# Shifting the activations by 32 bytes in SBUF: x and gg from 64 to 32 modulo 256

## The chip, the cores and the metric

The kernel runs on one core of a Trainium2 chip. The metric is the device time of one execution in microseconds. Three executions of the kernel before took 1003.8 to 1005.95 us, with a median of 1004.16 us.

## What is computed

Attention with a memory term, and then two feed-forward networks one behind the other, all in float32. This is the reference without its setup:

```python
scores = scale * q @ k.T;  causal mask;  a = softmax(scores);  local = a @ v
mem_out = (phi(q) @ M_prev) / (phi(q) . z_prev + 1e-06)
x = g * mem_out + (1 - g) * local          # 2304 tokens x 512
h = x @ w_in;   x = (s * max(h, 0)**2 + b) @ w_out          # layer 1, d_ff 2048
h = x @ w2_in
g = where(h >= 1, h, where(h <= -1, 0, (h + 1)**2 / 4))     # layer 2, d_ff 2048
out = g @ w2_out
```

## The kernel before

**Two halves of each number.** The large products run on TensorE as float32r. Each operand is split into a high and a low part, and each product is taken as three matmuls: high times high, high times low, low times high. So a matmul here reads a moving operand (the activations, 256 or 512 columns of 4 bytes in each of 128 partitions) and a stationary one (128 columns of weights, loaded by an LDWEIGHTS ahead of it).

**Stages.** From about 0 to 520 us attention (`att`) and layer 1 (`layer1`) are interleaved block by block after the table `ORDER`; a block is 256 tokens. The last block of layer 1 has 512 tokens ("wide", about 524 to 617 us). Layer 2 (`layer2`) follows to the end: its first products run by Strassen's scheme (`product`, lines 1181 to 1183, 256 columns; `plain`, lines 1235 to 1237, for the 256-token block), its second products (`second`, lines 1213, 1214, 1220; in `plain` lines 1252, 1254, 1255) have 512 columns.

**Which operand lies where.** Layer 1's first product (`h_mms`, lines 951 to 953) moves `xx`, which holds x in its high and low parts; the second (`layer1_step`, lines 1014, 1015 and 1019) moves `gg`, in the wide block alternately `gg` and `g2`. `product` moves the sums that layer 2 puts into `xx` and `gg` (`xo`), `plain` moves `xp`. The second products of layer 2 move weights (`wo`), with the activations as the stationary operand. The weights of all three are in tiles `wi` and `wo`.

Tiles are placed in SBUF one behind the other in the order in which the program makes them, each rounded up to 32 bytes. Tiles named `before_x`, `after_x` and `before_g2` hold nothing: they are there to set addresses. All offsets within these tiles at which a matmul of 256 or 512 columns begins are multiples of 1024 bytes (2048 for weights that move), so an operand's start modulo 256 is that of its tile. The start addresses per partition, modulo 256, as the built programs have them:

| tiles | what | before | after |
|---|---|---|---|
| `wi`, `wo`, `stg` | weights, staging | 128 | 128 |
| `xx` | x; layer 2's sums | 64 | 32 |
| `ident`, `zr`, `con` | constants | 128 | 96 |
| `mask`, `rr`, `gg` | mask; layer 1's activations | 64 | 32 |
| `qk`, `nv`, `zb`, `ee`, `uz` | attention's inputs, first steps | 64 | 32 |
| `pt`, `aa`, `at`, `au`, `av` | attention's scores and their transposes | 192 | 160 |
| `xp`, `xr`, `raw`, `st` | layer 2's inputs, staging of its weights | 64 | 32 |
| `g2` | layer 1's wide block; layer 2 | 128 | 128 |

The order of all instructions is worked out ahead by a planner (`Plan`) from a table of costs; every engine then runs its list in that order. Addresses are no part of that table.

Of the kernel before, what the change touches and what calls it, by code (L numbers as in the profile page):

```python
# [9 lines left out]
F32 = mybir.dt.float32  # L10
# [7 lines left out]
P = 128  # L18
# [357 lines left out]
def tile_kernel(ctx: ExitStack, tc: tile.TileContext, qk_in, nv_in, z_prev, beta,  # L376
# [16 lines left out]
    def t32(shape, name):  # L393
        return pool[0].tile(list(shape), F32, name=name)

    def t32r(shape, name):
        return pool[0].tile(list(shape), F32R, name=name)
# [17 lines left out]
    def w_out_part(i, j):  # L415
        return part("wo", i, j)
    stg_t = [t32([P, DM], f"stg{i}") for i in range(4)]
    t32([P, 48], "before_x")
    xx = t32r([P, 2 * NK * XC], "xx")
    xh = [xx[:, i * XC:(i + 1) * XC] for i in range(NK)]  # L420
    xl = [xx[:, (NK + i) * XC:(NK + i + 1) * XC] for i in range(NK)]
# [24 lines left out]
    TILES = [{}, {}]  # L446

    def pool_of(i, n, *parts):

        units = []  # L450
        for j in range(n):
            names = [f"{name}{i}{j}" for name, _, _ in parts]
            TILES[i].update({x: (shape, dt) for x, (_, shape, dt) in zip(names, parts)})
            units.append((lambda x=names[0]: made[x]) if len(names) == 1 else (lambda x=names: tuple(made[y] for y in x)))
        return Pool(units)
# [20 lines left out]
    TILES[1]["xr"] = ([P, NK * 2 * T], F32)  # L476
    R_RAW2 = pool_of(1, 3, ("raw", [P, 2 * DM], U32))
    R_STG2 = pool_of(1, 6, ("st", [P, DM], F32))
    TILES[1]["before_g2"] = ([P, 16], F32)
    TILES[1]["g2"] = ([P, 8 * T], F32R)  # L480


# [894 lines left out]
```

## Time and profile before

| what | value |
|---|---|
| median of three executions | 1004.16 us |
| the profiled execution, its own time | 1006.14 us |
| its span, first to last instruction | 1004.4 us |
| TensorE matmul busy | 992.5 us, 99% of the span |
| weight loads, beside the matmuls | 878.5 us |
| VectorE, ScalarE, GpSimd busy | 660.0, 589.0, 206.3 us |
| granted TensorE clock, mean | 0.995 |
| HBM traffic | 114 GB/s over the span |

The profiled execution's own time is 1.7 us above its span. Matmuls overlap in the records (the recorded length of one reaches past the start of the next), so what a matmul costs is read from the distance between the starts of two that follow each other, called its pitch below.

### The profile page before, as it was taken

The page shows a single profiled execution, that of the slowest core. Times are in us where ns is not written, and L with a number is a line of the kernel's source. Part 1 is how long each engine was busy: PE and PEld are TensorE (multiplying, and loading weights), DVE is VectorE, ACT ScalarE, POOL GpSimd, SP SyncE. Part 2 cuts the span into 40 slices and gives each one's busy share as a digit, 9 for nine tenths or more (in the row PEclk, how much of TensorE's full clock was granted, in tenths as well). Part 3 has the DMA queues.
Part 4 walks back from the last instruction along what each step waited for, and adds up shares of the span by engine and source line. Part 5 has one row for each costly group of instructions (what it writes and reads, how often), then busy time and mean ns, then how long its engine had stood idle before and what let it go on. Part 6 is the DMA issues. An engine that isn't in the chain of part 4 may idle for free.

```text
span 1004.4 us, 19651 instructions
## 1 busy us (share of the span) xinstructions
PE 992.5 (99%) x7480; PEld 878.5 (87%) x7480; DVE 660.0 (66%) x1545; ACT 589.0 (59%) x1331; POOL 206.3 (21%) x320
## 2 busy tenths in 40 slices
PE   8999999999999999999999999999999999999998
PEld 7799998898898889789898888999899998999987
DVE  5899855635644545554687885788769555576742
ACT  5999876646656655565556555666546434254323
POOL 5411133211110211111132321232234101011100
PEclk8999999999999999999999999999999999999999
DMA  9491034211221211211043334634354971231301
GB/s 321 170 410 60 15 92 140 70 52 49 76 70 48 85 62 56 68 60 46 1 152 132 127 116 143 225 126 147 110 185 162 355 248 46 82 95 32 106 27 37
DMA packets 50718, 115.57 MB, mean 115 GB/s; under 512 B 5440, under 2 KB 16192, under 8 KB 50624
## 3 DMA queue, kind: packets, MB, share of 16 engines
q1 hardware_dynamic: 50400, 113.73, 33.2%
q8 instruction: 59, 0.97, 0.4%
q0 software_dynamic: 224, 0.59, 0.3%
q14 instruction: 35, 0.29, 0.1%
HBM read 87.56 MB, written 26.74 MB: 114 GB/s over the span
## 4 chain that ended last, share of the span: by engine, by line
PE 91%; ACT 3%; DVE 2%; DMA 2%; issue 1%; SPq 0%; POOL 0%; DVEq 0%; POOLq 0%; ACTq 0%
PE hb L951 6%; PE hb L953 6%; PE hb L952 6%; PE ab L826 6%; PE yb L1014 5%; PE yb L1019 5%; PE yb L1015 5%; PE ab L905 4%; PE ab L881 4%; PE yb L1213 3%; PE yb L1214 3%; PE yb L1220 3%; PE ab L1220 3%; PE ab L1213 3%; PE ab L1214 3%; PE ab L1182 3%
## 5 line engine op out<-in xcount | busy, mean ns | idle before, releaser
L951 PE MATMUL hb<-xx,wi 128*128 128x256 f32 (+1 forms) x512 | 152.7, 298 | 0.0
L952 PE MATMUL hb<-xx,wi 128*128 128x256 f32 (+1 forms) x512 | 149.5, 292 | 0.0
L953 PE MATMUL hb<-xx,wi 128*128 128x256 f32 (+1 forms) x512 | 149.5, 292 | 0.0
L1014 PE MATMUL yb<-gg,wo 128*128 128x256 f32 (+1 forms) x394 | 102.6, 292 | 1.5 <-ACT gg L537 1.2
L951 PEld LDWEIGHTS hb<-xx,wi 128*128 128x128 f32 x512 | 96.4, 188 | 7.0 <-issue 3.5
L952 PEld LDWEIGHTS hb<-xx,wi 128*128 128x128 f32 x512 | 96.3, 188 | 2.8
L953 PEld LDWEIGHTS hb<-xx,wi 128*128 128x128 f32 x512 | 96.2, 188 | 2.9
L1015 PE MATMUL yb<-gg,wo 128*128 128x256 f32 (+1 forms) x394 | 98.0, 281 | 0.0
L522 ACT ACTIVATE aa<-aa,sm 128x384 f32<-128x384 f32 (+4 forms) x112 | 69.4, 621 | 48.2 <-DVE sm L837 48.0
L529 DVE TENSOR_TENSOR gg<-rr,gg 128x256 fp32r<-128x256 f32 (+1 forms) x102 | 44.6, 439 | 74.6 <-ACT gg L537 56.1
L1014 PEld LDWEIGHTS yb<-gg,wo 128*128 128x128 f32 x394 | 74.1, 188 | 9.0 <-issue 3.6
L837 DVE CUSTOM_DVE_ANT_0 aa<-ab,mask 128x512 f32<-128x512 f32 (+3 forms) x112 | 59.1, 553 | 32.9 <-PE ab L826 32.7
L995 ACT ACTIVATE rr<-hb 128x256 f32<-128x256 f32 (+1 forms) x105 | 42.8, 408 | 55.8 <-PE hb L953 52.8
L1015 PEld LDWEIGHTS yb<-gg,wo 128*128 128x128 f32 x394 | 74.2, 188 | 0.5
L1019 PE MATMUL yb<-gg,wo 128*128 128x256 f32 (+1 forms) x394 | 69.3, 288 | 0.0
L826 PE MATMUL ab<-qk 64*64 64x512 f32 (+5 forms) x320 | 58.4, 472 | 0.0
L1019 PEld LDWEIGHTS yb<-gg,wo 128*128 128x128 f32 x394 | 54.5, 188 | 2.4 <-issue 1.8
L861 POOL TENSOR_SCALAR aa<-aa,sm 128x384 f32<-128x384 f32 (+4 forms) x41 | 25.3, 619 | 149.1 <-DVE sm L854 114.8
L1182 PE MATMUL ab<-xx,wi 128*128 128x256 f32 x196 | 55.2, 282 | 0.0
L1181 PE MATMUL ab<-xx,wi 128*128 128x256 f32 x196 | 55.1, 281 | 0.0
L1183 PE MATMUL ab<-xx,wi 128*128 128x256 f32 x196 | 55.1, 281 | 0.0
L1181 PE MATMUL hb<-xx,wi 128*128 128x256 f32 x188 | 52.8, 281 | 0.0
(337 smaller groups left out, 2843.1 us busy)
## 6 DMA issues: line engine op xcount, KB each, us to landing
w2d<-st SPq DMA_DIRECT2D x48, 256.0 KB, 4.1
nv<-in_nv_dram SPq DMA_DIRECT2D x16, 576.0 KB, 3.7
wir<-in_moe_w_in_dram SPq DMA_DIRECT2D x16, 512.0 KB, 10.2
wor<-in_moe_w_out_dram SPq DMA_DIRECT2D x16, 512.0 KB, 10.2
raw<-in_moe_w_in_dram SPq DMA_DIRECT2D x16, 512.0 KB, 3.9
raw<-in_moe_w_out_dram SPq DMA_DIRECT2D x16, 512.0 KB, 4.4
qk<-in_qk_dram SPq DMA_DIRECT2D x16, 448.0 KB, 3.3
wo<-w2d SPq DMA_DIRECT2D x12, 512.0 KB, 5.1
```

The lines of the kernel that those rows point to most:

```text
L522: nc.scalar.activation(o(), i(), func, **{a: b() if callable(b) else b for a, b in kw.items()})
L826: nc.tensor.matmul(zs[x].t[own if t == 4 else slice(0, n), at:at + c1 - c0], qk.t[own, q0:q0 + n], qk.t[own, k0 + c0:k0 + c1], start=True, ...
L951: nc.tensor.matmul(o, w_in_part(fi, 0)[:, kt, :], x_h(kt), start=kt == 0, stop=False)
L952: nc.tensor.matmul(o, w_in_part(fi, 0)[:, kt, :], x_l(kt), start=False, stop=False)
L953: nc.tensor.matmul(o, w_in_part(fi, 1)[:, kt, :], x_h(kt), start=False, stop=kt == NK - 1)
L1014: nc.tensor.matmul(yv(c), w_out_part(fi, 0)[:, cs], gg.t[0], start=fi == 0 and c % k == 0, stop=False)
L1015: nc.tensor.matmul(yv(c), w_out_part(fi, 1)[:, cs], gg.t[0], start=False, stop=False)
L1019: pe(c_mm(n), lambda c=c, cs=cs, gg=gg, fi=fi: nc.tensor.matmul(yv(c), w_out_part(fi, 0)[:, cs], gg.t[1], start=False, stop=fi == NF - 1 a ...
L1181: nc.tensor.matmul(o, sw(q, k, 0, kt), xo(k, 0, kt), start=j == 0 and kt == 0, stop=False)
L1182: nc.tensor.matmul(o, sw(q, k, 0, kt), xo(k, 1, kt), start=False, stop=False)
L1213: nc.tensor.matmul(y.t, gh.t[:, cs], wo2(q, i, 0), start=first and jj == 0, stop=False)
L1214: nc.tensor.matmul(y.t, gh.t[:, cs], wo2(q, i, 1), start=False, stop=False)
```

## The change

The pad ahead of `xx` loses 8 float32 (32 bytes per partition), and the pad ahead of `g2` gains as many. So every tile from `xx` to the last one ahead of `before_g2` begins 32 bytes lower, and `g2` and the weights stay where they are. In the addresses after, `xx`, `rr`, `gg`, `xp` and the others of the table are at an odd multiple of 32 bytes.

```diff
     stg_t = [t32([P, DM], f"stg{i}") for i in range(4)]
-    t32([P, 48], "before_x")
+    t32([P, 40], "before_x")
     xx = t32r([P, 2 * NK * XC], "xx")
...
-    TILES[1]["before_g2"] = ([P, 16], F32)
+    TILES[1]["before_g2"] = ([P, 24], F32)
     TILES[1]["g2"] = ([P, 8 * T], F32R)
```

No instruction is added, removed or moved on any engine: the five engines' lists are the same row by row, and only operand addresses differ.

## Rows read from the trace of the kernel before

**Rows 1.** The page's first two parts: busy time by engine; 40 slices
```profile
PE 992.5 (99%) x7480; PEld 878.5 (87%) x7480; DVE 660.0 (66%) x1545; ACT 589.0 (59%) x1331; POOL 206.3 (21%) x320
...
PEclk8999999999999999999999999999999999999999
```

**Rows 2.** What TensorE waited for: us in total, times, longest
```profile
PE ab L826 <- DMA wir<-in_qk_dram: 3.2, 2, 1.7
PE yb L1014 <- ACT gg L537: 1.2, 1, 1.2
PE hb L1309 <- DVE zr L562: 1.1, 1, 1.1
...
PE yb L1014 <- POOL gg L542: 0.3, 1, 0.3
```

**Rows 3.** TensorE in time, layer 1: start, recorded length (us), line
```profile
295.76 0.28 PE L953 MATMUL hb<-xx,wi 128*128 128x256 f32 x1
...
297.12 0.28 PE L1014 MATMUL yb<-gg,wo 128*128 128x256 f32 x1
```

**Rows 4.** The same view, another stretch of layer 1
```profile
82.11 0.28 PE L1015 MATMUL ab<-gg,wo 128*128 128x256 f32 x1
...
83.99 0.28 PE L953 MATMUL hb<-xx,wi 128*128 128x256 f32 x1
```

**Rows 5.** The same view, layer 2: Strassen products, then second products
```profile
819.79 0.28 PE L1182 MATMUL hb<-xx,wi 128*128 128x256 f32 x1
...
823.21 0.39 PE L1213 MATMUL yb<-wo,wo 128*128 128x512 f32 x1
...
825.93 1.07 PE L1220 MATMUL ab<-wo,wo 128*128 128x512 f32 x4
```

**Rows 6.** The same view, layer 1's wide block: g2 is printed g
```profile
574.54 0.39 PE L1014 MATMUL yb<-g,wo 128*128 128x512 f32 x1
...
577.26 0.39 PE L951 MATMUL hb<-xx,wi 128*128 128x512 f32 x1
...
582.86 0.39 PE L1014 MATMUL yb<-gg,wo 128*128 128x512 f32 x1
...
585.66 0.39 PE L1014 MATMUL yb<-g,wo 128*128 128x512 f32 x1
```

**Rows 7.** Busy us (x instructions) by stretch: PE, PEld, DVE, ACT, POOL; clock; DMA
```profile
83.00:89.00 6.00, 6.00 (x53) 6.00 (x53) 5.70 (x11) 6.00 (x16) 1.08 (x1) 1.00 0.00 0
376.00:382.00 6.00, 6.00 (x53) 6.00 (x52) 1.71 (x4) 2.89 (x8) 0.51 (x1) 1.00 0.17 67
812.00:818.00 6.00, 6.00 (x53) 6.00 (x52) 2.33 (x4) 1.08 (x3) 0.00 (x0) 1.00 0.95 310
```

**Rows 8.** Groups by line and shape: count, busy us, mean recorded ns
```profile
L952 PE MATMUL hb<-xx,wi 128*128 128x256 f32 x448 | 124.3, 277 | 0.0
...
L1015 PE MATMUL yb<-gg,wo 128*128 128x256 f32 x384 | 94.1, 278 | 0.0
...
L1182 PE MATMUL ab<-xx,wi 128*128 128x256 f32 x196 | 55.2, 282 | 0.0
...
L952 PE MATMUL hb<-xx,wi 128*128 128x512 f32 x64 | 25.2, 394 | 0.0
...
L1235 PE MATMUL ab<-xp,wi 128*128 128x256 f32 x24 | 6.7, 281 | 0.0
...
L1015 PE MATMUL yb<-gg,wo 128*128 128x512 f32 x10 | 3.9, 394 | 0.0
```

## The prediction

> **What bounds the kernel.** I read the share of busy time first, then what TensorE waited for, then the starts of single matmuls. TensorE is busy for 992.5 of 1004.4 us, and its granted clock is full in all slices but the first [rows 1]. All its waits for other engines and for transfers come to 7.4 us; the largest are 3.2 us for the first inputs, 1.2 us for one gg, 1.1 us for a constant at the very start [rows 2]. So TensorE's own list is the path from end to end: a nanosecond on the pitch of a matmul is a nanosecond on the span, times the count, and a nanosecond on another engine is mostly nothing.
>
> The change leaves each instruction in its place, so what it can alter is how long an instruction takes at another address. The question is whether the trace shows a pitch that goes by address. It does, in two ways.
>
> First, by address. In the wide block the same line, L1014, runs with gg (64 modulo 256) and with g2 (128). With g2, 12 matmuls of 512 columns take 577.26 - 574.54 = 2.72 us, a pitch of 0.2267 us; with xx, 24 take 582.86 - 577.26 = 5.60 us, 0.2333 us; with gg, 12 take 585.66 - 582.86 = 2.80 us, 0.2333 us again [rows 6]. So 64 costs 6.7 ns a matmul more than 128, at 512 columns. Layer 2's second products, whose moving weights are at 128, also have 0.2267 us (12 in 825.93 - 823.21 us) [rows 5].
>
> Second, by state. At 256 columns and one address, 64, there are two pitches. In one stretch of layer 1, 12 matmuls with xx and gg take 297.12 - 295.76 = 1.36 us: 0.1133 us, half of 0.2267 [rows 3]. In another, with the same two tiles, 16 take 83.99 - 82.11 = 1.88 us: 0.1175 us [rows 4]. In layer 2, 29 take 823.21 - 819.79 = 3.42 us: 0.1179 us [rows 5]. I take 0.1177 us for the slow pitch, 4.4 ns over the fast one. A run of matmuls settles in one pitch and keeps it until something else interrupts it. Load elsewhere does not decide it: the slow pitch stands with VectorE and ScalarE full and DMA idle, with them idle and DMA at 0.95, and with all of them light [rows 7].
>
> How many stand in each, counted from the starts in that same view (between the first and last rows shown in [rows 3, 4] for layer 1, and like [rows 5] for layer 2): of layer 1's 2688 matmuls of 256 columns, 1678 at 114.5 ns or less, 784 slow, the rest in between or at the end of a run. Of layer 2's 1536, 1515 are slow. The recorded lengths agree: 281 to 282 ns in layer 2, and 277 to 278 ns as layer 1's mixed mean, with 394 ns for xx and gg in the wide block [rows 8]. So the slow pitch costs now 784 x 4.4 ns = 3.4 us in layer 1, 1515 x 4.4 ns = 6.7 us in layer 2, and 252 x 6.7 ns = 1.7 us in the wide block (192 with xx, 60 with gg).
>
> **The change part by part.** The pad ahead of xx moves xx, gg and xp from 64 to 32, so all of the 4224 matmuls of 256 columns and these 252 of 512 start at an address that no matmul of the trace before has: none of its starts is an odd multiple of 32. It is an operation whose cost must be bounded.
>
> From below: everything gets the pitch that the rows show for undisturbed runs, 0.1133 and 0.2267 us. That is - 3.4 - 6.7 - 1.7 = - 11.8 us.
>
> From above: every 256-column matmul pays over the fast pitch what the wide block's 512-column ones pay, 6.7 ns, so 0.1200 us. Layer 1: 1678 x 6.7 + 784 x 2.3 ns = 13.0 us; layer 2: 1515 x 2.3 ns = 3.5 us; the wide block, if it pays another 6.7 ns, 1.7 us. Sum + 18.2 us.
>
> In between lies the value that I take: at 32 the runs of layer 1 don't find the fast pitch any more, and all settle in the slow one, while layer 2 and the wide block stay as they are. That is 1678 x 4.4 ns = + 7.4 us. I choose it by the row that is nearest. From 128 to 64, the tile goes away from the weights' 128, and the 512-column rows get dearer by 6.7 ns [rows 6]; 32 is another step the same way. At 64 the fast pitch is already only one of two that a run can settle in, and coming out of the 512-column second products layer 2 never finds it [rows 5]. It is a choice: two addresses are no curve, and nothing in the trace says that a third lies on the line through them.
>
> What covers it: TensorE's waits in layer 1 for gg, 1.2 and 0.3 us [rows 2], shrink when the matmuls ahead of them take longer. I take 0.6 us of them as absorbed, between none and 1.7 us. Behind that nothing is late, as the engine was never short of ready work for longer.
>
> The other engines read and write at the new addresses too (rr, mask, aa, st), and the transfers land there. No row shows such an address, so their cost is bounded by who would feel it: TensorE's waits for ScalarE, VectorE and GpSimd. If these operations took longer by a tenth, the waits for gg might double, + 1.7 us; if shorter, they vanish, - 1.7 us. I take 0, since 7.4 us of waits in 1004 is what is left when the cover is that deep [rows 1, 2]. The transfers are waited for only at the start, 3.2 us [rows 2], into tiles that keep their address (wir); 0. The plain float32 matmuls of attention take the same addresses; half-way rows for them are missing as well, and I count 0, as no two pitches stand out there. The shift of g2's pad costs nothing: g2 stays at 128.
>
> The sum against the profiled execution is 1006.14 + 7.4 - 0.6 = 1012.9 us. That execution is 2.0 us above the median of the three runs, so against the median it is 1004.16 + 6.8 = 1011.0 us.
>
> **The rivals.** (1) Faster. The two pitches show that 64 is not a good address for layer 2, where a run that comes from the second products is caught in the slow pitch all the time [rows 5]. If from 32 such a run settles in the fast one, layer 2 gives 6.7 us: 997.5 us with layer 1 as it is; with layer 1 and the wide block too, 11.8 us: 992.4 us. It decides from the point at which layer 2's gain outweighs what layer 1's fast runs lose: with layer 1 all slow (+ 7.4) and layer 2 all fast (- 6.7) nothing would be left of it. For it: there is more slow than fast to win from now, 2299 matmuls against 1678. Against it: the only two addresses that can be compared get worse on the way down.
>
> (2) No change. The pitch may go by the 64 bytes in which the address lies, or by 128 and more, and not notice 32; then layer 2 is as slow, layer 1 as mixed: 1004.2 us, with about 1.5 us either way as runs of layer 1 fall otherwise. [...]
>
> (3) Slower by more: the bound above, 1004.16 + 18.2 = 1022.4 us, if an odd multiple of 32 costs each matmul one more step. That the change doesn't do what it says is no rival: the built program has the addresses of the table.
>
> **How the numbers follow.** All runs in the slow pitch, 1007 to 1015 us: 0.34, and 1011.0 us is the forecast. Slower by more, 1015 to 1022: 0.12. No change, 1002.2 to 1006.2: 0.18. Faster, 992 to 1002: 0.36, in which layer 2's gain alone (996 to 1000) is the larger part, and both layers' the smaller. A measurement of this kernel can tell 0.2% (2 us) from no change. So faster 0.36, same 0.18, slower 0.46. Both signs hold most of the chance, so the forecast's own range is 1007 to 1015; the range that should hold 8 in 10 leaves out the lowest part of the faster case (about 0.08) and the highest of the slower (about 0.09): 994 to 1017 us.
>
> **What would show it.** In the changed kernel's trace, the starts of L951 to L953 and L1014 to L1019 in undisturbed stretches of layer 1: 0.1177 us throughout by the forecast, some at 0.1133 by no change, 0.1200 by the third rival. Layer 2's L1181 to L1183: 0.1177 by the forecast, 0.1133 by the first rival. The wide block: xx and gg at 0.2333, and g2 at 0.2267 whatever happens; if g2 or the second products change, the pitch doesn't go by the moving operand's address at all. The forecast is wrong if layer 2 runs fast, or if waits for other engines grow beyond some 10 us, which would put the cause outside TensorE.

## The result: 0.8% slower, and where it shows in the profile after

The changed kernel takes 1012.59 us (median of 6, 1011.18 to 1014.89) against 1004.62 us before (median of 6): a ratio of 1.008, with a 95% interval of 1.0066 to 1.0094. That is 8.0 us slower; the forecast was 1011.0 us. The profiled execution has a span of 1010.2 us.

The page's busy times, and what TensorE waited for (us in total, times, longest), answer to [rows 1, 2]:

```profile
span 1010.2 us, 19651 instructions
PE 1000.9 (99%) x7480; PEld 887.7 (88%) x7480; DVE 660.4 (65%) x1545; ACT 589.6 (58%) x1331; POOL 204.8 (20%) x320
```
```profile
PE ab L826 <- DMA wir<-in_qk_dram: 1.6, 1, 1.6
PE hb L1309 <- DVE zr L562: 1.1, 1, 1.1
PE ab L796 <- POOL wor L788: 0.8, 1, 0.8
PE yb L1014 <- ACT gg L537: 0.5, 1, 0.5
```

VectorE, ScalarE and GpSimd are busy for as long as before, to 1.5 us; TensorE is busy for 8.4 us more, and its waits have shrunk, not grown: from 7.4 to 4.6 us in all, of which 1.6 us is the wait for the first inputs. So the time is in TensorE's matmuls themselves. TensorE in time, in a stretch of layer 1 that ran at 0.1133 us a matmul before, as in [rows 3]:

```profile
457.38 0.28 PE L952 MATMUL hb<-xx,wi 128*128 128x256 f32 x1
...
463.96 0.28 PE L1014 MATMUL yb<-gg,wo 128*128 128x256 f32 x1
```

56 matmuls in 6.58 us: 0.1175 us each. The same 56 took 6.35 us before, from 454.44 us on. No undisturbed run of layer 1 keeps 0.1133 us any more. Layer 2, the view of [rows 5]:

```profile
824.03 0.28 PE L1182 MATMUL ab<-xx,wi 128*128 128x256 f32 x1
824.16 0.28 PE L1183 MATMUL ab<-xx,wi 128*128 128x256 f32 x1
824.28 0.28 PE L1181 MATMUL ab<-xx,wi 128*128 128x256 f32 x1
824.39 0.28 PE L1182 MATMUL ab<-xx,wi 128*128 128x256 f32 x1
...
828.19 0.39 PE L1213 MATMUL yb<-wo,wo 128*128 128x512 f32 x1
```

35 in 4.16 us, 0.1189 us each; before it was 0.1179. The single steps are uneven: 0.13, 0.12, 0.11. Read to the nanosecond, the starts are 115 to 122 ns apart in a series that repeats, where the kernel before has 113 and 114 in its fast runs and 117 to 119 in its slow ones. In the wide block g2, which keeps its address, still reaches its pitch (a mean of 227.8 ns over its 132 matmuls, 228.0 before), and gg has got a little dearer, 234.1 ns against 233.3 (the view of [rows 6]):

```profile
566.48 0.62 PE L1019 MATMUL yb<-g,wo 128*128 128x512 f32 x2
566.93 0.62 PE L1019 MATMUL ab<-g,wo 128*128 128x512 f32 x2
567.39 0.40 PE L1014 MATMUL yb<-gg,wo 128*128 128x512 f32 x1
...
570.20 0.40 PE L951 MATMUL hb<-xx,wi 128*128 128x512 f32 x1
```

Four matmuls with g2 take 567.39 - 566.48 = 0.91 us (0.2275 us each), twelve with gg 570.20 - 567.39 = 2.81 us (0.2342).

The account of the 256- and 512-column products, from the starts of all matmuls of both traces. A pitch is the distance to TensorE's next start; distances over 140 ns (245 at 512 columns) are ends of runs and are left out of the means. The last row adds up those of layer 1.

| part | matmuls | before, mean ns | after, mean ns | us |
|---|---|---|---|---|
| layer 1, xx | 1291 | 114.66 | 117.78 | + 4.0 |
| layer 1, gg | 1234 | 115.07 | 117.95 | + 3.6 |
| wide block, xx and gg | 252 | 233.3 | 234.1 | + 0.2 |
| layer 2, first products | 1531 | 117.73 | 118.71 | + 1.5 |
| layer 2, second products | 855 | 226.86 | 227.26 | + 0.3 |
| ends of runs in layer 1 | 163 and 155 | 36.3 us | 33.4 us | - 2.9 |

The profiled pair's spans differ by 5.8 us and not by 8.0. The execution before is one that lies 2.0 us above its median, and following the same matmul through both traces shows where. At 25 us the changed kernel is 1.8 us ahead. Up to there the kernel before had waited 3.2 us for its first inputs, against 1.6 us, and its granted clock between 10 and 25 us was 0.77 of the full one, against 0.89. I put that lead down to the two executions and not to the change, since two experiments below with the old pitches, e1_others and e3_all_with_weights, lead the kernel before by 1.2 and 1.0 us at 25 us too. From there the changed kernel falls behind, to 3.9 us at 520 us, 4.1 us at 617 us and 5.8 us at the end. So it loses 5.7 us in the interleaved stages, 0.2 us in the wide block and 1.7 us in layer 2, 7.6 us together.

### The profile page after: what moved, and what is told of

Its sections match the earlier page's. It is cut to its first block, busy times and chain, and to the rows that moved or that the text cites. A ratio compares the mean times of both kernels' runs of the same rounds, so it can differ in the third digit from the quotient of the medians.

```text
span 1010.2 us, 19651 instructions
## 1 busy us (share of the span) xinstructions
PE 1000.9 (99%) x7480; PEld 887.7 (88%) x7480; DVE 660.4 (65%) x1545; ACT 589.6 (58%) x1331; POOL 204.8 (20%) x320
## 4 chain that ended last, share of the span: by engine, by line
PE 89%; ACT 6%; DVE 2%; DMA 2%; issue 1%; SPq 0%; DVEq 0%; POOL 0%
PE hb L951 6%; PE hb L952 6%; PE hb L953 6%; PE ab L826 6%; PE yb L1014 5%; PE yb L1019 5%; PE yb L1015 5%; PE ab L905 4%; PE ab L881 4%; PE yb L1213 3%; PE yb L1214 3%; PE yb L1220 3%; PE ab L1220 3%; PE ab L1213 3%; PE ab L1214 3%; PE ab L1182 3%
## 5 line engine op out<-in xcount | busy, mean ns | idle before, releaser
L1014 PE MATMUL yb<-gg,wo 128*128 128x256 f32 (+1 forms) x394 | 103.9, 294 | 0.5 <-ACT gg L537 0.5
L1015 PE MATMUL yb<-gg,wo 128*128 128x256 f32 (+1 forms) x394 | 99.8, 283 | 0.0
L1019 PE MATMUL yb<-gg,wo 128*128 128x256 f32 (+1 forms) x394 | 70.2, 290 | 0.0
```

Source lines behind the costliest of these rows:

```text
L1014: nc.tensor.matmul(yv(c), w_out_part(fi, 0)[:, cs], gg.t[0], start=fi == 0 and c % k == 0, stop=False)
L1015: nc.tensor.matmul(yv(c), w_out_part(fi, 1)[:, cs], gg.t[0], start=False, stop=False)
L1019: pe(c_mm(n), lambda c=c, cs=cs, gg=gg, fi=fi: nc.tensor.matmul(yv(c), w_out_part(fi, 0)[:, cs], gg.t[1], start=False, stop=fi == NF - 1 a ...
```

## Experiments

The question left was what the pitch goes by. **Theory A:** the loss comes from the operand that a matmul moves, either by its distance from the weights modulo 256 (A1) or by its own start, an odd multiple of 32 (A2). **Rival C:** it comes from the other engines or the transfers, whose arrays moved as well.

### All other arrays moved, xx, gg and xp not (e1_others)

```diff
-    t32([P, 16], "after_x")
+    t32([P, 8], "after_x")
...
+    t32([P, 8], "before_gg")
     gg_t = t32r([P, 6 * T], "gg")
...
+    TILES[0]["before_qk"] = ([P, 8], F32)
+    TILES[1]["after_xp"] = ([P, 8], F32)
-    TILES[1]["before_g2"] = ([P, 16], F32)
+    TILES[1]["before_g2"] = ([P, 8], F32)
```

> Only the arrays that no 256- or 512-column matmul moves go to odd multiples of 32 (rr, mask, constants, attention's arrays, layer 2's staging); xx, gg and xp stay at 64 modulo 256 and g2 and the weights at 128. Theory A, the loss comes from TensorE's moving operand: the time of the kernel before, within 2 us, and layer 1's 256-column matmuls at a mean of 115 ns with most of them at 113.3. Rival C, the loss comes from the other engines or the transfers at the new addresses: the 8 us loss of the changed kernel comes back, with layer 1's matmuls unchanged or TensorE waiting more.

Ratio 0.9997 (0.9987 to 1.0007). Layer 1 stands at 114.95 ns and layer 2 at 117.73. Rival C falls: that these arrays, which ScalarE, VectorE, GpSimd, the transfers and attention's matmuls touch, lie at odd multiples of 32 costs nothing that 0.1% would show. Attention's arrays are at 96 and 224 here and at 32 and 160 in the changed kernel; e4_weights_alone, below, has the loss with all of them where the kernel before has them.

### xx alone moved (e2_xx_alone)

```diff
-    t32([P, 48], "before_x")
+    t32([P, 40], "before_x")
...
-    t32([P, 16], "after_x")
+    t32([P, 24], "after_x")
```

> Only xx goes to 32 modulo 256; gg, xp and all else stay where the kernel before has them. If each matmul's pitch goes by its own operand's address: layer 1's matmuls with xx at 117.8 ns, those with gg at 115.0 as before, layer 2's with xx at 118.7; some 4.0 us in layer 1 and 1.2 us in layer 2 slower. If a run of matmuls settles as a whole: gg's go up too, as each run of xx's leads into one of gg's, and the loss is nearer to the 8 us of the whole change.

Ratio 1.0036 (1.0023 to 1.0049), 3.6 us. In layer 1 the matmuls with xx go to 117.86 ns, as in the changed kernel; those with gg, whose address is that of the kernel before, to 115.87, from 115.07. So in layer 1 the pitch goes by the operand that is moved, for the larger part. The 0.8 ns on gg is what runs of xx hand over to the runs behind them: it stands in the first matmuls of gg's runs, with 118.1 ns for the first of a run against 114.7 before, and is down to 0.5 ns by the ninth. In layer 2 the expectation missed: xx goes to 118.2 and not 118.7 ns, gg's matmuls, between those of xx, come down to 116.1 ns from 117.65 without having moved, and the two together lose 0.2 us instead of 1.2. So a matmul's own operand doesn't settle its pitch alone; what ran before it counts too.

### Everything moved, weights too (e3_all_with_weights), and the weights alone (e4_weights_alone)

```diff
+    t32([P, 56], "before_w")
     raws = {nm: [sb.tile([P, 2 * DM], U32, ...
```

> Every array, weights and g2 included, is 32 lower modulo 256 than in the kernel before (weights 96, xx, gg and xp 32, g2 96), so all distances between operands are those of the kernel before. Theory A1, the pitch goes by the distance of the moving operand's start from the weights' modulo 256: the time of the kernel before within 2 us, layer 1 at 115 ns, layer 2 at 117.75, and 226.7 ns for the 512-column products. Theory A2, a moving operand that starts at an odd multiple of 32 is dearer by itself: at least the 8 us loss, layer 1 at 117.8 ns, and the second products of layer 2, whose moving weights are now at 96, above 226.7 ns as well (855 of them; at 230 it would be another 2.8 us).

```diff
+    t32([P, 8], "before_w")
     raws = {nm: [sb.tile([P, 2 * DM], U32, ...
-    t32([P, 48], "before_x")
+    t32([P, 40], "before_x")
...
-    TILES[1]["before_g2"] = ([P, 16], F32)
+    TILES[1]["before_g2"] = ([P, 24], F32)
```

> The weights, their staging and g2 go up by 32, to 160 modulo 256; xx, gg and xp stay at 64, as in the kernel before. Theory A1 (distance from the weights): the distance is now 96 below, as in the changed kernel, so its pitches come back: 117.8 ns in layer 1, 118.7 in layer 2, some 8 us slower; the 512-column second products, whose two operands move together, stay at 226.7. Theory A2 (the moving operand's own start): layer 1 and layer 2's first products stay at 115.0 and 117.75 ns, and only the second products, which move weights at 160, may be slower.

With everything moved: ratio 0.9997 (0.9987 to 1.0006). With the weights alone: 1.0072 (1.0057 to 1.0087). TensorE in time in layer 1, first with everything moved, then with the weights alone:

```profile
298.73 0.28 PE L952 MATMUL hb<-xx,wi 128*128 128x256 f32 x1
...
301.45 0.28 PE L1015 MATMUL yb<-gg,wo 128*128 128x256 f32 x1
```
```profile
298.81 0.28 PE L1015 MATMUL yb<-gg,wo 128*128 128x256 f32 x1
...
301.42 0.28 PE L952 MATMUL hb<-xx,wi 128*128 128x256 f32 x1
```

The first has 24 matmuls with xx in 2.72 us, 0.1133 us each, with xx, gg, xp and the weights all at odd multiples of 32. The second has 22 with gg in 2.61 us, 0.1186 us each, with xx and gg where the kernel before has them. Over all undisturbed runs, layer 1 is at 114.95 and 117.89 ns, layer 2 at 117.77 and 118.71: the first pair is the kernel before's, the second the changed kernel's, to 0.15 ns. The second products, whose moving weights lie at an odd multiple of 32 in both, have 226.9 and 227.3 ns, again as before and as changed. That settles it for A1: what matters here is the distance between the start of the moving operand and that of the weights. The address itself, odd multiple of 32 or not, does not.

### Other distances (s0 to s224)

The pads were set so that xx, gg and xp begin at other places, with g2 and the weights at 128 modulo 256. For s0:

```diff
-    t32([P, 48], "before_x")
+    t32([P, 32], "before_x")
...
-    TILES[1]["before_g2"] = ([P, 16], F32)
+    TILES[1]["before_g2"] = ([P, 32], F32)
```

For s96, s128, s160, s192 and s224 the pair of pads is 56 and 8, none and 64, 8 and 56, 16 and 48, 24 and 40. For s48 and s80 the views begin 16 bytes into their tiles, and xp stays at 64:

```diff
-    t32([P, 48], "before_x")
-    xx = t32r([P, 2 * NK * XC], "xx")
+    t32([P, 40], "before_x")
+    xx = t32r([P, 2 * NK * XC + 8], "xx")[:, 4:4 + 2 * NK * XC]
...
-    t32([P, 16], "after_x")
+    t32([P, 8], "after_x")
...
-    gg_t = t32r([P, 6 * T], "gg")
+    gg_t = t32r([P, 6 * T + 8], "gg")[:, 4:4 + 6 * T]
```

(s80 keeps the pad of 48 and has one of 56 ahead of xp.)

> The arrays from xx to the phases' arrays begin 64 lower than in the kernel before: xx, gg and xp at 0 modulo 256, 128 below the weights' 128; g2 keeps its address. If the pitch at 256 columns rises with the distance below the weights (113.3 or 117.75 ns at 64, 117.8 to 118.7 at 96), it is 119 to 120 ns here and the time 1015 to 1020 us. If the distance acts by its place in a period of 256 and 64 and 96 are two places without order: anything from 113.3 ns (about 993 us) to 120.

> xx, gg and xp at 96 modulo 256, 32 below the weights. If the pitch rises with the distance below the weights: less than in the kernel before, layer 1 and layer 2 at 113.3 to 116 ns and 995 to 1002 us. If odd multiples of 32 of the distance keep runs from settling: a wandering pitch with a mean near 117.8 as at 96 below, and about 1012 us.

> xx, gg and xp at 128 modulo 256, level with the weights, as g2 and layer 2's moving weights are. By the 512-column products at that distance (226.7 ns, no exception in undisturbed runs) 256 columns would have 113.3 ns throughout: 11.8 us less than before, about 993 us. If what is best for 512 columns isn't for 256, the layer 1 and layer 2 products get dearer than 117.75 ns, and the time is above 1008 us; the wide block gains 1.5 us in either case.

> xx, gg and xp at 192 modulo 256, 64 above the weights. If only the size of the distance counts, it is as in the kernel before: 1004.5 us, with layer 2 at 117.75 ns. If its sign counts, the wide block's 233.3 ns and layer 2's pitch change, and the time is outside 1002 to 1007 us.

> The views of xx and gg begin 16 bytes into their tiles, at 48 modulo 256, 80 below the weights; xp, g2 and the weights as in the kernel before. So far 64 below is the cheapest distance, and 96 below loses 8 us. If the cost is smooth in the distance: between the two, layer 1 at 116 to 117 ns and about 1008 us. If 64 below is one exact place at which a run can settle at 113.3 ns: 117.5 ns or more, and 1010 to 1013 us. A gain below 1002 us would mean that the optimum lies between the 32-byte steps.

> xx and gg at 80 modulo 256, 48 below the weights; xp, g2 and the weights as in the kernel before. Smooth in the distance: between 64 below (1004.4 us) and 32 below (1012.2 us), about 1008 us. One exact place: 117.5 ns or more, 1010 to 1013 us. A gain below 1002 us would mean that the optimum lies between the 32-byte steps.

> xx, gg and xp at 160 modulo 256, 32 above the weights. If the distance acts in a period of 128 for 256 columns (64 above, 117.8 ns in layer 2, is like 64 below; level and 128 below are alike at 119.9): as at 96 below, 117.8 to 118.7 ns and about 1012 us. If above the weights the curve is another one, anything between 113.3 and 120 ns, 993 to 1016 us.

> xx, gg and xp at 224 modulo 256, 96 above the weights. In a period of 128 it is as at 32 below: 118.3 ns in both layers and about 1012 us. If not, anything between 113.3 and 120 ns, 993 to 1016 us.

The distance is the start of xx and gg less that of the weights, in bytes modulo 256; pitches are means in ns over undisturbed runs. In s48 and s80 layer 2's mean takes in 191 matmuls with xp, which stays at -64 and at 117.8 ns.

| kernel | distance | layer 1, 256 columns | layer 2, 256 columns | wide block, 512 | ratio to before (95%) |
|---|---|---|---|---|---|
| s0 | -128 | 118.8 | 119.9 | 233.0 | 1.0121 (1.0104 to 1.0138) |
| changed | -96 | 117.9 | 118.7 | 234.1 | 1.0080 (1.0066 to 1.0094) |
| s48 | -80 | 119.3 | 119.0 | 231.0 | 1.0108 (1.0093 to 1.0123) |
| before | -64 | 114.9 | 117.7 | 233.3 | 1 |
| s80 | -48 | 118.8 | 119.0 | 234.2 | 1.0102 (1.0086 to 1.0119) |
| s96 | -32 | 118.3 | 118.3 | 233.3 | 1.0080 (1.0065 to 1.0095) |
| s128 | 0 | 119.7 | 119.9 | 226.8 | 1.0118 (1.0103 to 1.0133) |
| s160 | +32 | 116.9 | 116.7 | 233.4 | 1.0033 (1.0020 to 1.0046) |
| s192 | +64 | 116.8 | 117.7 | 229.4 | 1.0036 (1.0023 to 1.0049) |
| s224 | +96 | 119.8 | 120.0 | 233.8 | 1.0138 (1.0123 to 1.0153) |

Three things follow. The curve is not smooth: -64 is a single place, and 16 bytes to either side of it cost over 10 us, more than 32 bytes do. s48, s80 and s224 came out dearer than any of their expectations had it (1015.5, 1015.4 and 1018.6 us). s48 and s80 are also the only ones whose moving operands start at an odd multiple of 16; no run moves the weights by 16 as well, so for these two it is not shown that the distance and not the start counts. So "smooth in the distance" falls, and so does a rise with the distance below the weights (-32 is as dear as -96). And there is no period of 128 either: +32 is cheap where -96 is not, and +96 is the dearest where -32 would make it 1012 us.

Second, 256 and 512 columns want different distances. Level with the weights, the wide block has its lowest pitch and the 256-column matmuls nearly their highest. TensorE in time, s128, in layer 1 and in the wide block:

```profile
304.81 0.28 PE L950 MATMUL hb<-xx,wi 128*128 128x256 f32 x1
...
306.85 0.64 PE L1018 MATMUL yb<-gg,wo 128*128 128x256 f32 x4
```
```profile
571.81 0.39 PE L1013 MATMUL yb<-gg,wo 128*128 128x512 f32 x1
...
573.62 0.62 PE L1018 MATMUL yb<-gg,wo 128*128 128x512 f32 x2
```

17 matmuls in 2.04 us are 0.1200 us each, without any wandering; 8 in 1.81 us are 0.2263 us each, with gg, which in the kernel before had 0.2333 [rows 6].

Third, only at -64 and at +64 do runs of layer 1 settle at 113.3 ns at all: 1678 of its 2688 matmuls stand at 114.5 ns or less at -64 and 543 at +64, in unbroken runs of up to 80 and 70. At the other distances runs wander, or settle at a dearer pitch. No place of these beats the kernel before. Layer 2 alone is 1.0 ns a matmul cheaper at +32 than at -64, which over its 1531 matmuls would be 1.5 us; a kernel with xx at -64 for layer 1 and layer 2's sums at +32 was not run.

## Why the prediction was right, and where its reason was not

- **The bound.** TensorE's list as the path from end to end held. Of 8.4 us more busy time on TensorE 5.8 show in the profiled span, where the execution before had lost 1.8 us at its start, and the medians differ by 8.0 us. No wait for another engine took over: all of TensorE's waits come to 4.6 us.
- **Layer 1's term.** Put at + 7.4 us, as 1678 fast matmuls that each lose 4.4 ns; it measured 4.0 + 3.6 = 7.6 us. The fast pitch is gone from layer 1, as forecast. What stands in its place is not the slow pitch of [rows 4] but a repeating series from 115 to 122 ns, whose mean, 117.9 ns, happens to be near it. That the size came out is luck: at the eight other distances the mean is anything from 116.8 to 119.8 ns.
- **Layer 2 and the wide block.** Put at 0; they measured + 1.5, + 0.3 (second products, whose first four in a run lose 5.3, 3.6, 1.9 and 1.9 ns) and + 0.2 us. "Layer 2 and the wide block stay as they are" was wrong by 2.0 us. From the thirteenth of a run on the second products are at 226.8 ns against 226.7, and g2 reaches its pitch, so the sign that the prediction set on these two, a change there, did not come.
- **What is absorbed.** Put at 0.6 us between 0 and 1.7. From 25 to 520 us the changed kernel loses 5.7 us against the kernel before, and 6.6 and 6.9 us against e1_others and e3_all_with_weights, which have the old pitches; the pitches of layer 1 alone make 7.6, 7.4 and 7.4 us. So between 0.5 and 1.9 us were absorbed, and single executions don't tell it closer. Layer 1's net loss thus lies at or somewhat under the forecast's 6.8 us, and the 8.0 us come from adding layer 2 and the wide block, which it left out.
- **The other engines.** Put at 0; e1_others shows it: 0.9997 (0.9987 to 1.0007).
- **The choice.** This is the step whose reason failed. It read from the 512-column rows that a tile gets dearer as it goes away from the weights' 128, and took 32 for another step the same way. But for 256 columns 128 is dearer than 64 by 4.8 ns in layer 1 (s128), 96 is dearer too, and 48 is dearer than 32. At 512 columns the rise doesn't go on either: 233.3 ns at 64, 234.1 at 32 and 233.0 at 0. The sign was right because 64 is the one place of ten at which most runs of layer 1 settle in the fast pitch, so that any other loses them; the row of 512 columns had no say in that. So the sign too was right for another reason than the one given. Nor does the pitch go by the moving operand's address alone, as the prediction has it: here it goes by that operand's distance from the weights (114.95 ns in layer 1 with the distance kept, e3_all_with_weights, and 117.89 with the weights alone moved, e4_weights_alone).
- **The rivals.** Faster, by layer 2 settling in the fast pitch, did not come: none of the ten distances does it for layer 2, whose lowest mean is 116.7 ns, at +32. No change, the second rival, did not come either: from 64 and from 32 the same lists take 1004.62 and 1012.59 us. The bound from above, every 256-column matmul at 0.1200 us, is what s128 has, with 119.7 and 119.9 ns, though at another address; its time is 1016.3 us (1.0118) and not the bound's 1022.4, since the wide block gains there instead of losing and the bound took nothing off for what is absorbed.

## What to carry to other kernels

Where TensorE has no idle time left, look at the distance of the starts of successive matmuls before and after a change of layout: pads in SBUF are part of this kernel's tuning, and 32 bytes taken from one of them and given to another cost it 0.8% (1012.59 us against 1004.62) without an instruction changed. Look at the moving operand's start against the weights' (here taken modulo 256), and try the places one by one for each number of columns, since here neither a neighbouring place nor the optimum for 512 columns told anything about 256: 16 bytes to either side of -64 cost over 10 us, and level with the weights 512 columns had 226.8 ns, their lowest, and 256 columns 119.7 ns. To find out what an effect of addresses hangs on, move one operand, then the other, then both.

## What the runs showed that was not expected

- In these kernels, whose executions had a mean granted clock of 0.994 to 1.0, a float32r matmul's pitch went with where its moving operand starts relative to its weights: 113.3 to 120.0 ns at 256 columns, 226.7 to 234.2 ns at 512, as means of one kernel or of one undisturbed run. Whether the period is 256 bytes was not tried: the distances run over 224 bytes, from -128 to +96.
- At one and the same distance, -64, 256-column runs have two lasting pitches, 113.3 and 117.8 ns, and which one a run takes went with what precedes it. In the kernel before, all 21 runs of 12 or more matmuls that begin straight behind a 512-column product are slow, and 48 of the 57 that begin behind a pause (a distance of over 140 ns) are fast; none of them changes over for good. Layer 2 can be fast too: its one such run behind a pause, in the middle of a series of slow products, has 12 matmuls in 1.36 us, 0.1133 us each. This is read from the traces; no run set the state on purpose, and what makes the other 9 slow is open.

```profile
759.70 0.28 PE L1181 MATMUL ab<-xx,wi 128*128 128x256 f32 x1
759.91 0.39 PE L1182 MATMUL ab<-xx,wi 128*128 128x256 f32 x1
...
760.61 0.28 PE L1181 MATMUL ab<-xx,wi 128*128 128x256 f32 x1
...
761.97 0.39 PE L1213 MATMUL ab<-wo,wo 128*128 128x512 f32 x1
```

- Why it is so stays open. The runs show, between -64 and -96, that the loss comes with the distance (1.0072 with the weights alone moved, 0.9997 with everything moved) and not with the arrays of the other engines and the transfers (0.9997 in e1_others); they don't show the mechanism.
